# RWKV-6 attention and a channel MLP on one core: TensorE's order written out, the MLP in steps between the levels

## The chip, the core and the metric

The kernel runs on one core of one Trainium2 chip. The metric is the device time of one execution in microseconds. TensorE (PE, with its weight loads as PEld) multiplies and transposes, VectorE (DVE), ScalarE (ACT) and GpSimd (POOL) do the elementwise work, SyncE (SP) issues most DMAs. Each engine runs its own instructions strictly in the order in which they were laid down for it; engines wait for each other by semaphores.

## The reference, cut to what matters

```python
# r, k, v, w: (4, 8, 768, 48) float32; u: (8, 48); d_model 384, hidden 1536
for t in range(S):                                  # attention, per batch and head
    cur = einsum('bhd,bhe->bhde', u[None] * kt, vt)
    y[:, :, t] = einsum('bhd,bhde->bhe', rt, state + cur)
    state = wt[:, :, :, None] * state + einsum('bhd,bhe->bhde', kt, vt)
x = y.transpose(0, 2, 1, 3).reshape(B, S, H * D)    # 8 heads x 48 = 384
xn = (x - mean(x)) / sqrt(var(x) + 1e-06) * g_ln
out = x + maximum(xn @ w_ch1, 0.0) @ w_ch2
```

The weights `w_ch1` and `w_ch2` arrive as float64 and are converted on the chip.

## The kernel before, in words

A **round** is half a sequence of one batch (384 time steps, all 8 heads); there are 8 of them, numbered 0 to 7. A round has two **units** of 4 heads. Per unit `load` (L103) fetches w, k and r, `turned` (L226) transposes them on TensorE (`w_ps`, `k_ps`, `r_ps`) with ACT copying the results out (L236), `totals` (L238) multiplies the decays pairwise on POOL, and `own_term` (L254) makes the u-term on POOL and DVE.

`level` (L280) is run six times per round, for both units at once. Level `lev` multiplies with TensorE (`a_ps`, 48 products), then DVE scales `rT` and `kT` in place for the next level (L304, four multiplies) and copies the masked products into `A` (L317, two masked copies, not in the last level, where ACT copies at L315). So a level's products wait for DVE's multiplies of the level before. After the last level `ends` (L327, `kn_ps`) transposes k back, `states` (L337, `kv` on TensorE, then a chain of small DVE operations at L360) carries the state from chunk to chunk, and `outputs` (L374) forms `y`.

`mlp` (L415) is the second half for one round: normalisation on DVE (L425 to L431), three groups of transposes (`xT_ps`, L439), then 36 products `h_ps` (L448) and 36 products `o_ps` (L457). In the trace each of these 72 products is two rows. It is a generator: each `yield` ends a step. `weights` (L188) is a generator too: each of its 24 steps converts one piece of the weights (two ACT, three DVE operations at L208, L212, L216, one POOL add at L220); `convert(n)` runs n steps.

Order: the loop of L498 to L533 lays round `rnd`'s levels, and between them round `rnd-1`'s states, outputs and MLP and round `rnd+1`'s transposes. The written order is a priority only: a scheduler orders each engine's instructions by it and by when it takes their inputs to be ready. Buffers: `ps_t` (2) for transposes, `ps_a` (2) for `a_ps`, `kv` and `y`, `ps_m` (2) for `xT_ps`, `h_ps` and `o_ps`.

## Time and profile before

| | |
|---|---|
| median of 3 runs | 666.06 us (664.53 to 671.01) |
| profiled execution, device time | 667.42 us |
| its span, first to last instruction | 665.7 us |
| TensorE busy | 603.3 us, 91% of the span |
| DVE, ACT, POOL busy | 300.4 us (45%), 193.3 us (29%), 145.4 us (22%) |
| mean granted TensorE clock | 0.93 of 2.4 GHz |
| chain that ended last | PE 79%, DVE 11%, issue 3%, DMA 3% |

Busy shares are means over very different stretches. The table by stretches below shows for each how long each engine was busy and which clock TensorE was granted (1.00 is 2.4 GHz, 0.50 is 1.2 GHz). A row of the chain gives start, duration, engine, output, line and number of merged instructions.

### The profile page before, as it was taken

What the parts mean: (1) busy time and instruction counts of PE and PEld (TensorE: products, weight loads), DVE (VectorE), ACT (ScalarE), POOL (GpSimd) and SP (SyncE); (2) the same over time, 40 slices, a digit from 0 to 9 for tenths busy, and PEclk for the clock granted to TensorE, in tenths of its full rate; (3) what the DMA queues carried; (4) which work ended last, traced back from release to release, by engine and by line L of the source; (5) the groups of instructions that cost most, each with busy time, mean ns of one, the idle gap of its engine ahead of it and who ended that gap; (6) DMA issues with size and microseconds to landing.
All of it is one profiled execution on the core that took longest, in us unless ns stands there. A gap on an engine that the chain in (4) does not pass through costs nothing.

```text
span 665.7 us, 19173 instructions
## 1 busy us (share of the span) xinstructions
PE 603.3 (91%) x8456; PEld 408.2 (61%) x8456; DVE 300.4 (45%) x683; ACT 193.3 (29%) x412; POOL 145.4 (22%) x195
## 2 busy tenths in 40 slices
PE   1785477999999999999999999999899989997997
PEld 0674365666756676566766675666656666664554
DVE  1589897736721486016731565035801491133000
ACT  3545345431323122231333123231323102321210
POOL 5837664540133004030133004030003000000000
PEclk9995576999999996999899998999999978998999
DMA  9845655611520035000530044001200000000000
GB/s 153 173 118 151 142 148 129 154 26 36 115 39 1 26 77 99 1 13 16 107 68 1 26 92 85 1 13 40 44 1 13 14 16 0 1 26 13 1 12 24
DMA packets 123251, 36.83 MB, mean 55 GB/s; under 512 B 116896, under 2 KB 120096, under 8 KB 123168
## 3 DMA queue, kind: packets, MB, share of 16 engines
q1 hardware_dynamic: 118368, 34.73, 23.8%
q10 hardware_dynamic: 4800, 0.89, 1.1%
q8 instruction: 66, 1.08, 0.7%
q14 instruction: 17, 0.14, 0.1%
HBM read 30.87 MB, written 4.72 MB: 53 GB/s over the span
## 4 chain that ended last, share of the span: by engine, by line
PE 79%; DVE 11%; issue 3%; DMA 3%; ACT 2%; POOL 1%; SPq 1%; ACTq 0%; DVEq 0%; POOLq 0%
PE h_ps L448 29%; PE o_ps L457 28%; PE a_ps L294 9%; PE xT_ps L439 2%; PE kv L348 2%; DVE kT L304 2%; DVE rT L304 2%; PE w_ps L232 2%; DVE A L317 2%; PE kn_ps L334 2%; PE r_ps L232 1%; PE k_ps L232 1%; PE y L387 1%; DVE stats L426 1%; PE y L403 1%
## 5 line engine op out<-in xcount | busy, mean ns | idle before, releaser
L448 PE MATMUL h_ps<-xT,w_sb 128*128 128x384 f32 x576 | 196.1, 502 | 0.0
L457 PE MATMUL o_ps<-w_sb,h 128*128 128x384 f32 x576 | 195.0, 490 | 0.0
L448 PEld LDWEIGHTS h_ps<-xT,w_sb 128*128 128x128 f32 x576 | 112.6, 198 | 77.7 <-issue 7.1
L457 PEld LDWEIGHTS o_ps<-w_sb,h 128*128 128x128 f32 x576 | 106.6, 190 | 68.1
L294 PE MATMUL a_ps<-rT,kT 48*64 48x32 f32 x4608 | 101.5, 236 | 11.3 <-DVE kT L304 6.4
L294 PEld LDWEIGHTS a_ps<-rT,kT 48*64 48x64 f32 x4608 | 91.0, 153 | 32.7 <-issue 16.7
L304 DVE TENSOR_TENSOR rT<-rT,tot 128x384 f32<-128x384 f32 x80 | 49.8, 623 | 128.5 <-PE a_ps L294 128.0
L452 ACT ACTIVATE h<-h_ps 128x384 f32<-128x384 f32 x96 | 47.0, 489 | 133.7 <-PE h_ps L448 133.5
L464 DVE TENSOR_TENSOR o<-o_ps,x 128x384 f32<-128x384 f32 x24 | 13.4, 559 | 123.7 <-PE o_ps L457 123.7
L275 POOL TENSOR_TENSOR vo<-v,own 128x576 f32<-128x576 f32 x16 | 19.8, 1239 | 178.2 <-DMA v<-in_v_dram 165.4
L317 DVE COPY_PREDICATED A<-mask,a_ps 128x384 f32<-128x384 int8 x80 | 54.8, 749 | 0.0
L304 DVE TENSOR_TENSOR kT<-kT,tot 128x384 f32<-128x384 f32 x80 | 53.2, 666 | 0.0
L360 DVE SCALAR_TENSOR_TENSOR s<-s,decay,kv 128x48 f32<-128x48 f32 x160 | 29.4, 258 | 25.4 <-PE kv L348 25.4
L250 POOL TENSOR_TENSOR tot<-wT 128x384 f32<-128x384 f32 x16 | 14.8, 926 | 110.5 <-DVE kT L304 110.5
L220 POOL TENSOR_TENSOR w_sb<-we,wl 128x384 int32<-128x384 int32 x24 | 28.5, 1196 | 33.3 <-DVE we L216 24.7
L259 POOL TENSOR_TENSOR rk<-nat_k,nat_r 128x576 f32<-128x576 f32 x16 | 26.3, 1644 | 41.7 <-DMA nat_r<-in_r_dram 16.0
L369 ACT COPY sx<-s 64x288 f32<-64x288 f32 x32 | 13.8, 430 | 73.7 <-DVE s L360 73.4
L270 DVE TENSOR_REDUCE own<-rk 128x12 f32<-128x576 f32 x16 | 12.0, 749 | 46.2 <-POOL rk L264 46.2
L335 ACT COPY kn<-kn_ps 128x384 f32<-128x384 f32 x32 | 14.0, 481 | 52.3 <-PE kn_ps L334 38.9
L232 PE MATMUL k_ps<-ident,nat_k 128*128 128x128 f32 x96 | 18.7, 341 | 10.5 <-ACT wT L236 10.5
L439 PE MATMUL xT_ps<-ident,xn 128*128 128x128 f32 x72 | 18.7, 373 | 10.1 <-DVE xn L431 9.0
L403 PE MATMUL y<-sx,rx 48*64 48x48 f32 x384 | 24.5, 222 | 1.8 <-issue 1.8
(57 smaller groups left out, 599.4 us busy)
## 6 DMA issues: line engine op xcount, KB each, us to landing
raw<-in_moe_w_ch_dram SPq DMA_DIRECT2D x24, 384.0 KB, 3.6
v<-in_v_dram SPq DMA_DIRECT2D x64, 72.0 KB, 2.4
out_dram<-o SPq DMA_DIRECT2D x24, 192.0 KB, 1.9
nat_w<-in_w_dram SPq DMA_DIRECT2D x60, 72.0 KB, 2.9
nat_k<-in_k_dram SPq DMA_DIRECT2D x60, 72.0 KB, 3.1
nat_r<-in_r_dram SPq DMA_DIRECT2D x60, 72.0 KB, 2.6
vx<-in_v_dram SPq DMA_DIRECT2D x64, 36.0 KB, 2.3
nat_w<-in_w_dram ACTq DMA_DIRECT2D x4, 72.0 KB, 3.4
```

Source lines behind the costliest of these rows:

```text
L220: POOL.tensor_tensor(out=dst.bitcast(I32), in0=e, in1=low, op=ALU.add)
L232: PE.transpose(ps[:, ts(c, P)], nat[nm][q % 2][:, pr * TT + c].rearrange("p j d -> p (j d)"), ident,)
L259: POOL.tensor_tensor(out=rk, in0=nat["k"][q % 2][:, :, :, 0:D], in1=nat["r"][q % 2][:, :, :, 0:D], op=ALU.mult,)
L294: PE.matmul(ps[ds(C * (i ^ j), C), j, uu, c].rearrange("s (q n) -> s q n", n=n), K[rows, ts(m, C)], R[rows, m, :, 1, :], start=True, stop= ...
L304: DVE.tensor_tensor(out=X, in0=X, in1=T[:, :, 1 - i][:, :, None].broadcast_to(blocks), op=ALU.mult,)
L317: DVE.copy_predicated(out=out_j[:, :, 1, :], mask=masks[lev], data=ps_j)
L360: DVE.scalar_tensor_tensor(out=s[:, pr, m, :], in0=s[:, pr, m - 1, :] if m else before[:, pr, 2 * TT - 1, :], scalar=a["T"][NLEV][:, c : c ...
L403: PE.matmul(y[ds(C * i, C), j, k_], R, s, start=False, stop=True, skip_group_check=True,)
L439: PE.transpose(ps[:, ts(i, P)], xn[i].rearrange("p h d -> p (h d)")[:, ts(kc, P)], ident)
L448: PE.matmul(ps, w1_sb[:, kc, ts(f, P)], xT[:, kc, :], start=kc == 0, stop=kc == KC - 1)
L452: ACT.activation(out=hs[f], in_=ps, func=AF.Relu)
L457: PE.matmul(ps.rearrange("p h d -> p (h d)"), hs[f][:, ts(i, P)], w2_sb[:, f, :], start=f == 0, stop=f == FC - 1,)
```

## The change

- All TensorE instructions are kept in the written order (`keep_in_program_order`); the scheduler still places the other engines' instructions.
- Round 0 runs alone: levels, `ends`, `states`, `outputs`, normalisation and `xT` of its MLP are laid down before round 1's first level, with only round 1's transposes between them.
- The MLP's products are handed out by `fill` as 24 steps of three products. MLP 0 is spread over 11 levels (round 1's six and round 2's first five), every later MLP over six levels, and the transposes of the next round, of `kn` and of `xT` go one by one between these steps.
- `norm`, `turned_x` and `mlp` are separate; `xT_ps` uses `ps_t`; `ends` moves to the last level of its own round; the last level's ACT copies are collected in `late` and laid down by `finish`.
- The masks are kept once (32 columns) and broadcast when read; POOL makes them instead of ACT. The first loads go to SP and, for one of six, to ACT; the square root's table is loaded at the start. The converter's buffers come from the pool of `h`. Weights are converted three pieces per level from round 1.

```diff
+    def matmul(*args, **kw):
+        tc.keep_in_program_order(PE.matmul(*args, **kw))
+
+    def transpose(*args):
+        tc.keep_in_program_order(PE.transpose(*args))
...
-    load(0)
-    load(1, ACT)
+    load(0, (SP, SP, ACT))
+    load(1)
+    eps = const.tile([P, 1], F32, name="eps")
+    DVE.memset(eps, 1e-6)
+
+    ACT.activation(out=const.tile([P, 1], F32, name="root"), in_=eps, func=AF.Sqrt)
...
-        half = const.tile([P, U * NK, C // 2], I8, name=f"mask{lev}")
+        half = const.tile([P, C // 2], I8, name=f"mask{lev}")
...
-            ACT.copy(
-                out=half[rows],
-                in_=m[rows, None, ds(C // 2 * i, C // 2)].broadcast_to([C, U * NK, C // 2]),
-            )
...
+            POOL.tensor_copy(out=half[rows], in_=m[rows, ds(C // 2 * i, C // 2)])
...
-                    ACT.copy(out=out_j[rows, :, 1, :], in_=ps_j[rows])
+                    late.append((out_j[rows, :, 0, 1, :], ps_j[rows, :, 0]))
...
-                DVE.copy_predicated(out=out_j[:, :, 1, :], mask=masks[lev], data=ps_j)
+                mask = masks[lev][:, None].broadcast_to([P, U * NK, C // (2 * n), n])
+                DVE.copy_predicated(out=out_j[:, :, :, 1, :], mask=mask, data=ps_j)
...
-    MLP_STEPS = 2 + FC + TT * ((FC - 1) // 3 + 1)
+    MLP_STEPS = FC + TT * (FC // KC)
...
+    def fill(until, tasks):
+
+        n = int(until) - done
+        for i in range(max(n, len(tasks))):
+            if i < len(tasks):
+                tasks[i]()
+            for _ in range((i + 1) * n // max(n, len(tasks)) - i * n // max(n, len(tasks))):
+                mlp_step()
...
+    for part, nm in ((0, "w"), (1, "k"), (2, "r"), (3, None)):
+        (states if part < U else outputs)(now[part % U])
+        if nm:
+            for task in all_turned(new, nm):
+                task()
+    norm(0)
+    for task in all_x(0):
+        task()
...
+    FIRST = 2 * NLEV - 1
+    for rnd in range(1, NR + 1):
+        old, now, new = units_of(rnd - 1), units_of(rnd), units_of(rnd + 1)
         for lev in range(NLEV):
...
+            slot = (rnd - 1) * NLEV + lev + 1
+            until = MLP_STEPS * (
+                slot / FIRST if slot <= FIRST else 1 + (slot - FIRST) / NLEV
+            )
+            if rnd > 1 and lev < 2 * U:
+                (states if lev < U else outputs)(old[lev % U])
+                if lev == 2 * U - 1:
+                    norm(rnd - 1)
...
+            if lev == 4:
+                if rnd > 1:
+                    tasks = all_x(rnd - 1)
...
+            if lev == 5 and now:
+                tasks = [lambda: None] * 2 + all_ends(now)
+            fill(until, tasks)
+            if lev == 4 and rnd > 1:
+                mlps.append(mlp(rnd - 1))
```

**ACT at the start of the program, before** (`nat_` are the loaded operands, `mask_` the masks, `wT` the transposed decays of unit 0):

```order
L106 DMA nat_r_90<-in_r_dram 128x3x48 x4
L162 ACT_TABLE_LOAD
L162 COPY mask_148<-mask_0_144 64x384 x2
L162 COPY mask_155<-mask_1_151 64x384 x2
L162 COPY mask_162<-mask_2_158 64x384 x2
L162 COPY mask_169<-mask_3_165 64x384 x2
L162 COPY mask_176<-mask_4_172 64x384 x2
L236 COPY wT_183<-w_ps_0_184 128x384
L236 COPY wT_183<-w_ps_1_189 128x384
```

ACT at the start of the program, now:

```order
L112 DMA nat_r_89<-in_r_dram 128x3x48 x4
L135 ACT_TABLE_LOAD
L135 ACTIVATE root<-eps 128x1
L241 COPY wT_185<-w_ps_0_186 128x384
L241 COPY wT_185<-w_ps_1_191 128x384
```

Eight of ACT's twelve transfers have gone to SP, and ten mask copies stand no longer ahead of the first copy of a transposed operand.

**TensorE from MLP 0's last transpose on, before** (`a_ps_4` is level 4 of round 1):

```order
L439 MATMUL xT_ps_0_2_1350<-ident,xn_0_2_1324 128x128
L448 MATMUL h_ps_0_0_1377<-xT_0_1325,w_sb 128x384 x3
L448 MATMUL h_ps_0_1_1383<-xT_0_1325,w_sb 128x384 x3
L448 MATMUL h_ps_0_2_1474<-xT_0_1325,w_sb 128x384 x3
L448 MATMUL h_ps_0_3_1480<-xT_0_1325,w_sb 128x384 x3
L448 MATMUL h_ps_0_4_1528<-xT_0_1325,w_sb 128x384 x3
L448 MATMUL h_ps_0_5_1534<-xT_0_1325,w_sb 128x384 x3
L448 MATMUL h_ps_0_6_1540<-xT_0_1325,w_sb 128x384 x3
L294 MATMUL a_ps_4_1576<-rT_631,kT_534 64x32 x24
L294 MATMUL a_ps_4_1576<-rT_642,kT_545 64x32 x24
```

TensorE from MLP 0's last transpose on, now (`a_ps_0` is round 1's level 0, `w_ps` belongs to round 2):

```order
L59 MATMUL xT_ps_2_1071<-ident,xn_0_2_1045 128x128
L56 MATMUL a_ps_0_1116<-rT_972,kT_903 64x32 x24
L56 MATMUL a_ps_0_1116<-rT_983,kT_914 64x32 x24
L56 MATMUL h_ps_0_0_1195<-xT_1060,w_sb 128x384 x3
L56 MATMUL h_ps_0_1_1201<-xT_1060,w_sb 128x384 x3
L56 MATMUL a_ps_1_1237<-rT_972,kT_903 64x32 x24
L56 MATMUL a_ps_1_1237<-rT_983,kT_914 64x32 x24
L59 MATMUL w_ps_0_1293<-ident,nat_w_85 128x128 x3
L59 MATMUL w_ps_1_1298<-ident,nat_w_85 128x128 x3
L56 MATMUL h_ps_0_2_1303<-xT_1060,w_sb 128x384 x3
```

Before, four levels of round 1 had been laid down ahead of MLP 0 and its steps followed in one piece; now MLP 0's transposes stand ahead of all of round 1's levels, and two steps stand between two levels.

**TensorE in round 2 between levels 3 and 4, before**:

```order
L294 MATMUL a_ps_3_2316<-rT_1497,kT_1366 64x32 x24
L232 MATMUL r_ps_0_2390<-ident,nat_r_89 128x128 x3
L232 MATMUL r_ps_1_2395<-ident,nat_r_89 128x128 x3
L294 MATMUL a_ps_4_2443<-rT_1486,kT_1355 64x32 x4
L232 MATMUL r_ps_0_2401<-ident,nat_r_90 128x128 x3
L294 MATMUL a_ps_4_2443<-rT_1486,kT_1355 64x32
L232 MATMUL r_ps_1_2406<-ident,nat_r_90 128x128 x3
L294 MATMUL a_ps_4_2443<-rT_1486,kT_1355 64x32 x19
```

The same place now (`o_ps` are MLP 0's products):

```order
L56 MATMUL a_ps_3_2262<-rT_1557,kT_1428 64x32 x24
L59 MATMUL r_ps_0_2328<-ident,nat_r_89 128x128 x3
L59 MATMUL r_ps_1_2333<-ident,nat_r_89 128x128 x3
L56 MATMUL o_ps_0_1_2054<-w_sb,h_0_9_1675 128x384
L56 MATMUL o_ps_0_1_2054<-w_sb,h_0_10_1736 128x384
L56 MATMUL o_ps_0_1_2054<-w_sb,h_0_11_1753 128x384
L59 MATMUL r_ps_0_2345<-ident,nat_r_90 128x128 x3
L59 MATMUL r_ps_1_2350<-ident,nat_r_90 128x128 x3
L56 MATMUL o_ps_0_2_2355<-w_sb,h_0_0_1199 128x384
```

Before, only transposes stood between the two levels, since MLP 0's products had all been laid down by then; now two steps of MLP 0 stand there.

## Rows read from the trace of the kernel before

**Rows 1.** Page, part 1: busy us of TensorE, share, instructions.

```profile
PE 603.3 (91%) x8456; PEld 408.2 (61%) x8456; DVE 300.4 (45%) x683; ACT 193.3 (29%) x412; POOL 145.4 (22%) x195
```

**Rows 2.** Table by stretches: limits, length, busy us (instructions) by engine, clock, DMA.

```profile
core 0: us, PE busy (x) PEld busy (x) DVE busy (x) ACT busy (x) POOL busy (x), PEclk, DMA share, GB/s
0.00:29.00 29.00, 10.76 (x82) 7.77 (x83) 8.79 (x12) 13.47 (x27) 19.00 (x42) 1.00 1.07 175
29.00:109.00 80.00, 54.86 (x1281) 46.07 (x1282) 72.03 (x144) 36.38 (x79) 45.24 (x44) 0.68 0.54 134
109.00:184.00 75.00, 73.86 (x1162) 49.43 (x1162) 45.94 (x101) 25.61 (x56) 23.42 (x27) 0.98 0.41 89
184.00:258.00 74.00, 72.97 (x1046) 49.29 (x1044) 31.02 (x77) 19.95 (x44) 13.14 (x19) 0.94 0.22 45
...
551.00:614.00 63.00, 58.09 (x552) 36.58 (x551) 14.46 (x46) 15.06 (x32) 0.00 (x0) 0.96 0.03 11
```

**Rows 3.** Chain that ended last, one round and the end: start, us, what.

```profile
183.66 23.41 PE h_ps L448 x72
207.07 1.53 PE a_ps L294 x96
...
231.89 0.84 PE kv L348 x48
...
234.12 1.49 PE o_ps L457 x4
237.16 2.78 PE o_ps L457 x8
239.94 0.66 PE w_ps L232 x6
...
551.35 21.94 PE h_ps L448 x66
...
614.04 24.95 PE h_ps L448 x72
639.00 23.23 PE o_ps L457 x72
```

**Rows 4.** Table by stretches, at one end of a round (columns as above).

```profile
249.00:262.00 13.00, 13.00 (x131) 9.04 (x127) 9.47 (x18) 3.84 (x8) 4.15 (x3) 0.50 0.65 123
```

**Rows 5.** Timeline at the start (start, us, queue); last row: page 6, us to landing.

```profile
10.32 1.28 ACT L162 ACT_TABLE_LOAD   x1 [10.32 <-DMA nat_r<-in_r_dram]
11.62 3.11 ACT L162 COPY mask<-mask 64x384 int8<-64x384 int8 x6
...
17.01 0.86 ACT L236 COPY wT<-w_ps 128x384 f32<-128x384 f32 x2
...
19.60 1.97 SPq L106 DMA_DIRECT2D nat_k<-in_k_dram  x4
...
nat_r<-in_r_dram SPq DMA_DIRECT2D x60, 72.0 KB, 2.6
```

**Rows 6.** Groups by line, DVE: count, busy us, mean ns, idle before.

```profile
L317 DVE COPY_PREDICATED A<-mask,a_ps 128x384 f32<-128x384 int8 x80 | 54.8, 749 | 0.0
L304 DVE TENSOR_TENSOR kT<-kT,tot 128x384 f32<-128x384 f32 x80 | 53.2, 666 | 0.0
L212 DVE TENSOR_SCALAR we<-we 128x384 int32<-128x384 int32 x24 | 14.1, 592 | 0.2
```

**Rows 7.** Timeline, DVE's first levels and POOL beside them.

```profile
29.03 0.87 DVE L304 TENSOR_TENSOR rT<-rT,wT 128x384 f32<-128x384 f32 x1 [1.18 <-PE a_ps L294]
...
32.62 1.77 DVE L304 TENSOR_TENSOR kT<-kT,wT 128x384 f32<-128x384 f32 x1
...
36.96 0.55 DVE L304 TENSOR_TENSOR kT<-kT,tot 128x384 f32<-128x384 f32 x1
...
32.54 1.43 POOL L259 TENSOR_TENSOR rk<-nat_k,nat_r 128x576 f32<-128x576 f32 x1 [0.48 <-DMA nat_r<-in_r_dram]
```

**Rows 8.** Waits of TensorE: for whom, us in total, times, longest.

```profile
PE xT_ps L439 <- DVE xn L431: 9.0, 5, 4.7
```

More of the change, by code (lines that the diff above doesn't have):

```diff
@@ L224, with turned @@
     st, carry = {}, {}
[L226 removed]
+    def turned(q, nm, pr):
         a = st.setdefault(q, {})
[L228 to L236 removed]
+        if pr == 0:
+            a[nm] = (p2 if nm == "w" else p4).tile([P, W], F32, tag=nm, name=f"{nm}T{q}")
+        ps = ps_t.tile([P, RN], F32, tag="t", name=f"{nm}_ps{q}_{pr}")
+        for c in range(TT):
+            transpose(
+                ps[:, ts(c, P)],
+                nat[nm][q % 2][:, pr * TT + c].rearrange("p j d -> p (j d)"), ident,
+            )
+        ACT.copy(out=a[nm][:, ts(pr, RN)], in_=ps)
     def totals(q):
@@ L478, in convert, with mlp_step @@
             next(ws, None)
-    for q in range(U):
+    mlps, done = [], 0
+    def mlp_step():
+        nonlocal done
+        while mlps:
+            if next(mlps[0], mlps) is not mlps:
+                done += 1
+                return True
+            mlps.pop(0)
+        return False
+    def fill(until, tasks):
[5 more added lines that the diff above has]
+                mlp_step()
@@ L481, with all_turned, all_ends, all_x @@
+    def all_turned(qs, nm):
+        return [lambda q=q, pr=pr: turned(q, nm, pr) for q in qs for pr in range(NP)]
+    def all_ends(qs):
+        return [lambda q=q, pr=pr: ends(q, pr) for q in qs for pr in range(NP)]
+    def all_x(rnd):
+        return [lambda kc=kc: turned_x(rnd, kc) for kc in range(KC)]
+    def units_of(rnd):
+        return [U * rnd + g for g in range(U)] if rnd < NR else []
+    now, new = units_of(0), units_of(1)
+    for q in now:
         for nm in "wkr":
-            turned(q, nm)
+            for task in all_turned([q], nm):
+                task()
@@ L483 @@
         totals(q)
-    for q in range(U):
+    for q in now:
         own_term(q)
-    mlps, owed = [], 0.0
-    def mlp_steps(n):
-        nonlocal owed
-        owed = owed + n if mlps else 0.0
-        while mlps and owed >= 1.0:
-            if next(mlps[0], mlps) is mlps:
-                mlps.pop(0)
-            else:
-                owed -= 1.0
-    RATE = 1.05 * MLP_STEPS / NLEV
-    for rnd in range(NR + 1):
-        now, old, new = (
-            [U * i + g for g in range(U)] if 0 <= i < NR else [] for i in (rnd, rnd - 1, rnd + 1)
-        )
-        for lev in range(NLEV):
-            if old and lev == 0:
-                for q in old:
-                    ends(q)
-            if old and lev in (0, 1):
-                states(old[lev])
+    for lev in range(NLEV):
+        level(now, lev)
+        if lev == 0:
+            for q in now:
+                load_vx(q)
+        if lev == 1:
+            for q in new:
+                load(q)
+        convert(2)
@@ L517 @@
                     load(q)
-            if lev in (1, 2, 3):
-                for q in new:
-                    turned(q, "wkr"[lev - 1])
+            tasks = []
+            if new and lev in (1, 2, 3):
+                tasks = all_turned(new, "wkr"[lev - 1])
             if lev == 3:
```

128 lines of the change are left out of this document (65 added, 63 removed).

## The prediction

> **What bounds the kernel now.** I read the page's busy line first: TensorE is busy 91% of the span [rows 1]. That is a mean, so the table by stretches comes next, and there three regimes are to be seen [rows 2]. Up to 29 us almost nothing but loading happens, with the DMA engines full. From 29 to 109 us DVE is the bound, 72.0 of 80 us, while TensorE has 54.9, mostly at 1.2 GHz (clock 0.68): the only TensorE work at hand is that of the levels, whose products each wait for DVE. From 109 us on, when MLP 0's products are there, TensorE is busy nearly throughout. The chain then shows what one round is made of [rows 3]: from 183.66, where MLP 1's products begin, to 239.94 it is dense; behind that the MLP has run out, and the rest of the round is levels and transposes that wait for DVE, with pauses, and in the round shown with the clock at 0.50 for 13 us although TensorE counts as fully busy [rows 4]. At the round's end TensorE waits for the normalisation, 9.0 us over five places [rows 8].
>
> From 183.66 to MLP 6's start at 551.35 there are five rounds, 73.5 us each; MLP 6's round has 62.7, and MLP 7 48.2 up to the last product at 662.2 [rows 3]. Behind that are 3.5 us to the end of the span at 665.7, and 1.7 us lie between the span and the device time of 667.4. The profiled execution is 1.4 us above the median of 666.06.
>
> **The start.** ACT copies the first transposed operand at 17.01: until 10.32 it stood behind its own loads, then came the table and ten mask copies [rows 5]. DVE's first level began at 29.03 [rows 7]. Now ACT issues 4 transfers and copies at once. Unit 1's r, the last operand that level 0 needs, is the twentieth transfer on SP; four took 1.97 us there [rows 5], so issuing ends at some 11 us, landing 2.6 later [rows 5] at 13.5, and two transposes, a copy and half a level put DVE's first multiply at about **17 us** (estimate): 12 earlier.
>
> The Trainium skill, page "Trainium Kernel Development and Optimization", Key Constraints, says that transfers from all queues share the same 16 DMA engines and that more issuing engines save only issue time. By it the move of transfers from ACT to SP brings no datum earlier; the trace agrees as far as it goes, with a DMA share of 1.07 from both queues in the first stretch [rows 2].
>
> Up to MLP 0's products DVE has the work of the stretch from 29 to 109 without two parts: four of round 1's levels, which now stand behind MLP 0's transposes, and four of 16 conversions (12 are laid down ahead now). A level has four multiplies of 0.67 and two masked copies of 0.75 [rows 6], 4.1 us; a conversion has three operations of about 0.59, 1.77 us. So 72.0 - 16.4 - 7.1 = 48.5 us of DVE remain; at the same nine tenths busy that is 54, and I add 6 for the chain `kn`, `kv`, `y`, normalisation, `xT`, which has no level beside it any more. MLP 0 starts at 17 + 54 + 6 = **77 us** instead of 109 (bounds 70 and 84).
>
> **Eleven levels beside MLP 0.** Now two or three of MLP 0's 24 steps stand between two levels. A step is three products, 6 rows; 72 rows take 23.41 us [rows 3], so 1.95. TensorE's part of one of the first five levels is 1.53 + 3.9 + 1.3 for transposes (six take 0.66, 239.94 in rows 3) and some joints, 7.1 us. DVE's is 4.1 + three conversions, 5.3, together 9.4 in four of the five: there DVE stays the bound, and the early start is partly waited away. 8 + 4 x 9.4 = 45.6. With these pauses the clock is open; the nearest rows are 0.68 [rows 2] and 0.50 [rows 4]. Never low costs nothing; always low makes a level 14 us of TensorE, 19 more in four. I take 6. The sixth level has three steps and `kn`, 9 us. The next five hold 11 steps (21.5), levels 7.6, `kv` 1.7, two `y` at 1.55 (the gap before 237.16 in rows 3) plus joints 3.5, transposes 5.2: 39.5, and 3 where the normalisation joins the level on DVE. So the point that stood at 183.66, MLP 0 done and level 4 of round 2 too, comes at 77 + 51.6 + 9 + 42.5 = **180 us** (160 to 204). The start gains 3 us only: MLP 0 no longer runs in one dense piece.
>
> DVE's own operations are the softest number. One multiply took 1.77 us while POOL's 1.43 ran beside it, another 0.55 [rows 7]. Without such meetings DVE's part falls below TensorE's and the point comes near 160. The Trainium skill, page "SBUF — State Buffer", Who interferes with whom, says that DVE and GpSimd share a port pair as an exclusive lock, so that the later one waits for the whole of the other's instruction. The trace agrees in that one meeting (0.55 + 1.2 against 1.77). If each of the 12 POOL adds of the conversions beside these levels held DVE up by that 1.2, the sum would be some 14 us longer.
>
> **The rounds behind it.** One round at full clock without pauses is 56.3 (183.66 to 239.94) plus what is left: three levels 4.6, transposes 4.0, a `y` 1.75, `xT` 1.0: 67.6. So 4 x 67.6, one round without new transposes at 63.6, MLP 6's round with 56 and MLP 7 with 46.6 are 436.6, against 478.6 now: 42 us lie in these ends of rounds. The order now puts four steps, 7.8 us, between any two levels, and the next MLP begins at level 5 where the last one ends at level 4; so the wait for DVE (4.1 us per level, 31.0 per round of 74 [rows 2]) has cover, and without cover it would be back. I give back 6 for some ten more joints per round (about 0.12 each, from 1.49 for four `o_ps` rows against 0.32 each) and 9 for the level with the normalisation, and for ACT's copies at the sixth, 1.5 per round. Gain **27 us**: 451.6 remain.
>
> Costed at nothing: the broadcast mask (same element count; if its reading doubled the copy, 1.5 us in each of 10 DVE-bound levels, 15 us, otherwise covered); ten small copies on POOL, about 0.52 each by ACT's 3.11 for six [rows 5], ahead of work that starts at 7 us; `kn` at two buffers; out transfers, which wait behind loads on SP but have two buffers. The square root's table, 1.28 us at 10.32 [rows 5], is loaded ahead of the work.
>
> **Sum.** 180 + 451.6 + 3.5 = 635 us of span, 637 with the 1.7 outside it.
>
> **Rivals.**
> - *DVE does not bind in the first levels.* For it speaks 0.55 us per multiply alone [rows 7]; against it the mean of 0.67 over all rounds [rows 6]. The point comes at 160: 617 us.
> - *The strict order brings the wait back.* A TensorE instruction that waits now holds up everything behind it, MLP steps too; before, the scheduler had placed the products behind the levels. The place is the level with the normalisation: DVE has a `y` addition, the normalisation and four multiplies there, about 8 us (estimate, operations of 0.5 to 0.8), against 10.6 on TensorE (1.53 + 7.8 + 1.3). Meetings with POOL, or ACT's copies at the sixth level, could turn that into 3.5 to 4 us of pause per round, 22 in all: 659 us, hardly a change.
> - *The clock falls in every round* (the other side). At 249 us it was at 0.50 with TensorE fully busy on transposes and levels [rows 4]; these now stand in among the steps. For 13 us per round at half clock 6.5 us are lost, 39 in six rounds: 676 us, slower. It decides from 6 us per round on. Against it: the dense part of rows 3 has levels, `kv` and `y` between pieces of 1.5 to 9 us of MLP and ran at the price of full clock.
>
> **How the numbers follow.** A change under 1% can't be told from none here, so the limits are 659.4 and 672.7. Forecast 0.64, DVE not binding 0.17, wait brought back 0.12, clock in every round 0.07. Nearly all of the first, all of the second and a third of the third are faster: 0.81; the rest of the third and some of the first within 1%: 0.12; slower 0.07. The range goes from 614 (first rival, less 3) to 664 (start at its upper bound, 24 more, or the strict order's 659 with some of it); the clock's case is left out.
>
> **What would show it.** In the profile after: DVE's first level near 17 us; MLP 0's first product near 77 and MLP 1's near 180; DVE busy nine tenths up to 130; in the later rounds TensorE busy over 97% with clock near 1.00 and rounds of about 70 us instead of 73.5; the wait of `xT_ps` for DVE nearly gone. Wrong would be: a new wait of `a_ps` or `kn_ps` of more than 2 us per round; a clock under 0.9 in rounds 3 to 7; or a start of MLP 1 beyond 200, which would mean that the spread of MLP 0 costs more than the earlier start gives.

## The result, and the profile after

The changed kernel takes 629.41 us (median of 4 runs, 629.00 to 630.72), against 665.82 us for the kernel before, run beside it (664.53 to 671.01): a ratio of 0.945, with a 95% interval of 0.940 to 0.950. Medians, here and below, are of all runs of a kernel; ratios leave out the runs of a slower state, more than 1.5% above the kernel's fastest, which the kernel before and e4 show. The forecast was 637 us, between 614 and 664. The profiled execution of after has a span of 628.1 us.

Engines' busy time (page, part 1), to be laid beside [rows 1]:

```profile
PE 573.4 (91%) x8456; PEld 387.2 (62%) x8456; DVE 303.2 (48%) x683; ACT 185.2 (29%) x402; POOL 152.4 (24%) x205
```

TensorE's share is the same 91%, which shows how little that number says. Its 8456 products and transposes are the same, and their busy time fell from 603.3 to 573.4 us; idle time fell only from 62.4 to 54.7. Most of the gain is TensorE being quicker at the same work.

Stretches of after, cut at the marks that the forecast used (first product of MLP 0, of MLP 1, then round by round; columns as in [rows 2]):

```profile
0.00:17.00 17.00, 9.70 (x132) 6.83 (x132) 2.73 (x3) 7.03 (x14) 12.61 (x45) 1.00 0.79 141
17.00:85.00 68.00, 37.71 (x901) 32.28 (x901) 55.36 (x116) 26.28 (x56) 42.73 (x43) 0.59 0.66 152
85.00:182.00 97.00, 88.75 (x1598) 61.26 (x1595) 69.77 (x141) 35.89 (x80) 44.83 (x38) 0.92 0.47 104
182.00:254.00 72.00, 69.53 (x1051) 46.55 (x1052) 34.90 (x83) 20.55 (x45) 13.28 (x18) 0.98 0.23 49
254.00:321.00 67.00, 67.00 (x1066) 45.41 (x1065) 33.30 (x75) 20.03 (x45) 13.41 (x18) 1.00 0.25 50
321.00:389.00 68.00, 67.11 (x1050) 45.35 (x1048) 33.69 (x79) 19.74 (x45) 13.16 (x18) 1.00 0.24 49
524.00:578.00 54.00, 54.00 (x453) 33.42 (x452) 11.41 (x40) 14.50 (x32) 0.00 (x0) 1.00 0.03 10
```

From MLP 1 on TensorE hardly rests and holds 2.4 GHz. Ahead of MLP 0 the picture is the old one: DVE busy 55.4 of 68 us, TensorE mostly at 1.2 GHz.

Chain that ended last, marks of after (start, us, what), beside [rows 3]:

```profile
85.39 6.61 PE h_ps L56 x12
...
181.91 2.15 PE h_ps L56 x6
184.61 1.94 PE h_ps L56 x6
...
253.64 2.13 PE h_ps L56 x6
...
578.18 23.22 PE h_ps L56 x72
601.40 23.23 PE o_ps L56 x72
```

MLP 0 begins at 85.4 (before some 109), MLP 1 at 181.9 (183.7), and the last product ends at 624.6 (662.2). So only 2 us are won up to MLP 1, and 36 behind it: 442.7 us remain from there instead of 478.5.

The same two stretches, before (184 to 662) and after (182 to 625):

```profile
184.00:662.00 478.00, 463.63 (x5934) 304.92 (x5932) 173.12 (x427) 117.88 (x253) 57.75 (x84) 0.96 0.14 30
```

```profile
182.00:625.00 443.00, 437.25 (x5838) 286.81 (x5838) 175.08 (x425) 115.97 (x252) 52.25 (x80) 0.99 0.14 31
```

The idle part went from 14.4 to 5.8 us, the busy part from 463.6 to 437.3, with 1.6% fewer records in the second (one level of round 2, some 1.5 us, stands ahead of MLP 1's start now). Part of the difference is the clock, 0.96 against 0.99. An estimate: if a mean of 0.96 stands for 8% of the time at half clock and 0.99 for 2%, that is up to 19 and 4 us lost, so up to 15 of the 26. The rest shows in a round of before that had full clock throughout, from MLP 3's start to MLP 4's. TensorE is busy for 69.7 us there; the same round of after, 321 to 389 above, has as many records and needs 67.1:

```profile
335.00:406.00 71.00, 69.72 (x1050) 47.01 (x1049) 31.64 (x79) 20.29 (x44) 13.15 (x18) 1.00 0.26 52
```

What TensorE does there in before, at the end of the MLP (timeline, PE; two transposed operands and levels 2 and 3 in turns):

```profile
396.57 0.39 PE L294 MATMUL a_ps<-rT,kT 48*64 48x32 f32 x10 [0.20 <-DVE A L317]
396.89 0.87 PE L232 MATMUL k_ps<-ident,nat_k 128*128 128x128 f32 x6
397.69 1.48 PE L294 MATMUL a_ps<-rT,kT 48*64 48x32 f32 x86
399.10 0.87 PE L232 MATMUL r_ps<-ident,nat_r 128*128 128x128 f32 x6
400.52 0.32 PE L294 MATMUL a_ps<-rT,kT 48*64 48x32 f32 x8 [0.54 <-DVE kT L304]
400.77 0.55 PE L232 MATMUL r_ps<-ident,nat_r 128*128 128x128 f32 x3
401.24 0.30 PE L294 MATMUL a_ps<-rT,kT 48*64 48x32 f32 x2
```

Levels are broken up between transposes: 8 rows of `a_ps` take 0.32 us there, while an unbroken level of 96 takes 1.39 to 1.6, so 8 would be 0.13. The end of one row overlaps the next, so starts are the better measure: 0.25 us from the start of the 8 rows to that of the transposes, and 0.47 for the three transposes, which take 0.33 between steps of the MLP (step 5 further down). The break costs some 0.26 us. In the trace behind MLP 1's start `a_ps` stands in 63 pieces for 31 levels before, and now in one piece per level but for a few rows beside `y`; at 0.2 to 0.26 us for each of 32 breaks that is 6 to 8 us (estimate). With the clock's 15 and the level's 1.5 that makes most of the 26. The groups of TensorE's rows from MLP 1's start to the last product point the same way, though they hold the clock's part too; before, then after (columns as in [rows 6]):

```profile
L294 PE MATMUL a_ps<-rT,kT 48*64 48x32 f32 x2976 | 61.1, 227 | 5.0 <-DVE A L317 3.0 <-DVE mv L427 0.9 <-DVE kT L304 0.5
L439 PE MATMUL xT_ps<-ident,xn 128*128 128x128 f32 x55 | 14.6, 374 | 6.1 <-DVE xn L431 5.5 <-ACT xT L442 0.2
```

```profile
L56 PE MATMUL a_ps<-rT,kT 48*64 48x32 f32 x2888 | 50.0, 219 | 4.4 <-issue 4.4
L59 PE MATMUL xT_ps<-ident,xn 128*128 128x128 f32 x54 | 9.1, 278 | 0.0
```

### The profile page after: what moved, and what is told of

It is laid out like the page before. It is cut to its first block, busy times and chain, and to the rows that moved or that the text cites. A ratio compares the mean times of both kernels' runs of the same rounds, so it can differ in the third digit from the quotient of the medians.

```text
span 628.1 us, 19238 instructions
## 1 busy us (share of the span) xinstructions
PE 573.4 (91%) x8456; PEld 387.2 (62%) x8456; DVE 303.2 (48%) x683; ACT 185.2 (29%) x402; POOL 152.4 (24%) x205
## 4 chain that ended last, share of the span: by engine, by line
PE 82%; DVE 8%; issue 3%; DMA 2%; POOL 2%; SPq 2%; ACT 1%; POOLq 0%; DVEq 0%; ACTq 0%
PE h_ps L56 30%; PE o_ps L56 29%; PE a_ps L56 10%; PE y L56 4%; PE kv L56 2%; PE r_ps L59 2%; PE kn_ps L59 2%; SPq L112 2%; DVE we L221 1%; PE w_ps L59 1%; PE xT_ps L59 1%; DMA nat_r<-in_r_dram 1%; DVE kT L309 1%; PE k_ps L59 1%; DVE rT L309 1%
## 5 line engine op out<-in xcount | busy, mean ns | idle before, releaser
L56 PE MATMUL h_ps<-xT,w_sb 128*128 128x384 f32 x576 | 202.1, 499 | 2.2 <-ACT h L475 2.2
L56 PE MATMUL o_ps<-w_sb,h 128*128 128x384 f32 x576 | 201.2, 495 | 0.0
L56 PEld LDWEIGHTS o_ps<-w_sb,h 128*128 128x128 f32 x576 | 106.4, 194 | 61.3 <-issue 3.0
L56 PE MATMUL a_ps<-rT,kT 48*64 48x32 f32 x4608 | 86.8, 229 | 25.8 <-DVE kT L309 20.2
L56 PEld LDWEIGHTS a_ps<-rT,kT 48*64 48x64 f32 x4608 | 81.2, 146 | 37.4 <-issue 19.7
L309 DVE TENSOR_TENSOR kT<-kT,tot 128x384 f32<-128x384 f32 x80 | 60.2, 752 | 0.0
L421 DVE TENSOR_TENSOR x<-y,vo 128x576 f32<-128x576 f32 x16 | 12.1, 757 | 61.6 <-PE y L56 61.6
L460 ACT ACTIVATE xT<-xT_ps,g_sb 128x384 f32<-128x384 f32 x24 | 13.9, 580 | 58.5 <-PE xT_ps L59 58.5
L241 ACT COPY rT<-r_ps 128x384 f32<-128x384 f32 x32 | 14.6, 477 | 50.7 <-PE r_ps L59 50.7
L241 ACT COPY kT<-k_ps 128x384 f32<-128x384 f32 x32 | 14.8, 478 | 43.9 <-PE k_ps L59 43.8
L56 PEld LDWEIGHTS y<-v,A 64*64 64x64 f32 x384 | 21.8, 138 | 8.1 <-issue 7.1
```

Of the source, the lines that this page charges most:

```text
L56: tc.keep_in_program_order(PE.matmul(*args, **kw))
L241: ACT.copy(out=a[nm][:, ts(pr, RN)], in_=ps)
L309: DVE.tensor_tensor(out=X, in0=X, in1=T[:, :, 1 - i][:, :, None].broadcast_to(blocks), op=ALU.mult,)
L460: ACT.activation(out=xTs[rnd][:, kc, :], in_=ps, func=AF.Copy, scale=g_sb[:, kc : kc + 1])
```

## The experiments

"First level" is DVE's first multiply, "rest" the time from MLP 1's first product to the end of the last product, all from one profile each; times are medians. Kernels whose code ahead of MLP 0 is the same as after's begin it at 85.4, 88.6 and 88.8, and e2, whose code is that of after up to MLP 1, begins MLP 1 at 185.1 instead of 181.9: a mark is good to about 3 us. Each ratio is to the kernel before as run beside that kernel. There were three such groups after the first comparison, each on a chip of its own: e1 to e4; e5, e9, e11, e12; e6, e7, e20, e22. After itself was run in none of them, and the kernel before has medians of 664.57 to 667.11 in them. So a difference of 3 or 4 us between kernels of different groups, or to after, is not shown by the medians alone.

| kernel | time, us | ratio to before (95%) | first level | MLP 0 | MLP 1 | rest |
|---|---|---|---|---|---|---|
| before | 665.82 | 1 | 29.0 | 108.7 | 183.7 | 478.5 |
| after | 629.41 | 0.945 (0.940 to 0.950) | 24.1 | 85.4 | 181.9 | 442.7 |
| e1_free_order | 630.57 | 0.956 (0.950 to 0.961) | 18.1 | 87.1 | 183.1 | 439.9 |
| e2_one_piece | 711.47 | 1.078 (1.071 to 1.084) | 24.0 | 88.8 | 185.1 | 521.3 |
| e11_mlp0_behind | 641.00 | 0.968 (0.962 to 0.974) | 24.1 | 126.0 | 197.0 | 441.7 |
| e6_mlp0_dense | 640.54 | 0.964 (0.959 to 0.969) | 24.1 | 93.7 | 195.8 | 440.5 |
| e3_old_start | 634.23 | 0.962 (0.957 to 0.967) | 31.0 | 96.4 | 191.1 | 438.7 |
| e4_new_start_alone | 664.16 | 0.997 (0.991 to 1.003) | 18.1 | 108.5 | 186.8 | 479.9 |
| e5_own_later | 621.84 | 0.940 (0.935 to 0.944) | 15.6 | 83.1 | 177.3 | 439.8 |
| e22_own_pinned | 625.21 | 0.940 (0.935 to 0.946) | 24.1 | 84.2 | 179.5 | 439.5 |
| e7_conversion_cut | 627.93 | 0.944 (0.939 to 0.949) | 24.1 | 88.6 | 183.0 | 440.9 |
| e9_convert_later | 630.48 | 0.953 (0.948 to 0.958) | 24.1 | 82.4 | 185.2 | 439.1 |
| e12_both | 630.21 | 0.952 (0.948 to 0.958) | 15.6 | 80.2 | 184.4 | 439.0 |
| e20_raw_ahead | 631.88 | 0.950 (0.943 to 0.956) | 15.6 | 86.2 | 192.7 | 439.0 |

The kernel before scatters more than after (657 to 685 us in the later comparisons), which widens the intervals. The profiles of e11 (643.89 us) and e20 (637.19) are of the slowest of their runs, that of e4 (671.94) is of one near its slowest.

### Are the steps between the levels what counts, or the pins?

**e2_one_piece:** MLP 1 to 7 in one piece each; everything else, pins too, as in after.

```diff
-                slot / FIRST if slot <= FIRST else 1 + (slot - FIRST) / NLEV
+                slot / FIRST if slot <= FIRST else 1 + -(-(slot - FIRST) // NLEV)
```

> MLP 1 to MLP 7 are handed out in one piece of 24 steps at the slot where the next one of the six begins, instead of four steps per level; MLP 0 as it was. Theory (an uncovered level waits for DVE): five of six gaps between levels have no TensorE work but transposes, DVE's 4.1 us per level show as waits of a_ps, less the 0.7 to 1.3 us of transposes: some 12 us per round over six rounds with levels beside them, 680 to 705 us. Rival (what counts is that TensorE's order is pinned and the next MLP begins at level 5; the waits would be short because DVE works ahead of TensorE): under 645 us.

Measured 711.47 us, 82 more than after and more than the kernel before. MLP 1 begins at 185.1, and the rest is 79 us longer. The stretch from MLP 1's start to the last product, and one end of a round:

```profile
185.10:706.40 521.30, 481.24 (x5844) 323.35 (x5838) 171.43 (x425) 116.93 (x252) 51.25 (x80) 0.90 0.12 26
```

```profile
235.00:265.00 30.00, 23.39 (x874) 20.50 (x866) 25.32 (x71) 9.02 (x20) 2.67 (x2) 0.89 0.41 80
```

The theory is right against the rival, but its sum is not: it had some 12 us of waits in each of six rounds and nothing for slower products. In the 30 us without steps DVE is busy for 25.3 and TensorE for 23.4. Over the whole rest TensorE is idle for 40 us instead of 5.8 and busy for 44 us longer, at a clock of 0.90. Of the waits of `a_ps`, 13.0 us are put down to DVE's chain of states `s`, 3.7 to its multiplies and 1.6 to its masked copies: it is DVE's whole work between two levels that shows, and not the multiplies alone. So an uncovered level is paid for twice, about half in waits and half in slower products; and the pinned order without the steps is worse than what the free scheduler made of the kernel before.

**e1_free_order:** the pins taken away, the order still written as in after.

```diff
-        tc.keep_in_program_order(PE.matmul(*args, **kw))
+        PE.matmul(*args, **kw)
...
-        tc.keep_in_program_order(PE.transpose(*args))
+        PE.transpose(*args)
```

> Only the pins are taken away: TensorE's instructions are written in the same order, but the scheduler may move them again. Theory (the gain of the later rounds comes from steps of the MLP standing between the levels; the pin only keeps what is written): the scheduler moves some transposes and levels forward, most steps stay between the levels: 625 to 645 us. Rival (the pin carries the gain, since a free scheduler gathers the MLP's products into one dense piece again, as in the kernel before): rounds go back towards 73 us, 650 to 665 us, with a_ps waiting for DVE again by 4 us at several levels of each round.

Measured 630.57 us (628.19 to 631.97): by the medians no difference that these runs can tell from after's 629.00 to 630.72. The ratios, 0.956 and 0.945, would allow the pins some 7 us (estimate), their intervals just touch. The theory is right, the rival out: the rest is 439.9 us, no longer than after's. The scheduler leaves the steps where they are written; the clearest move is at the start, where it takes most of two levels of round 1 ahead of MLP 0's transposes. The pin is not where the gain comes from.

One thing stays open. The kernel before was not in one piece: its steps stood between levels until they ran out. How much of the 36 us is the even spread, and how much the rest of TensorE's new order (transposes one by one between steps, `ends` in its own round, `xT_ps` in other buffers), was not run apart.

### What the first MLP's place is worth

**e11_mlp0_behind:** round 0's states, outputs and normalisation between round 1's levels, MLP 0 over six levels, as in later rounds.

```diff
-    for part, nm in ((0, "w"), (1, "k"), (2, "r"), (3, None)):
-        (states if part < U else outputs)(now[part % U])
...
-    mlps.append(mlp(0))
...
-                slot / FIRST if slot <= FIRST else 1 + (slot - FIRST) / NLEV
+                max(0, slot - NLEV + 1) / NLEV
...
-            if rnd > 1 and lev < 2 * U:
+            if lev < 2 * U:
```

> Changed kernel without the first MLP's chain ahead of round 1's levels: round 0's states, outputs, normalisation and transposes stand between round 1's first five levels as in later rounds, and MLP 0 is handed out over six levels instead of eleven. Theory (round 1's first five levels then have no steps beside them and are bound by DVE at about 9 us each, while the chain of states is covered): MLP 0's first product at 112 to 122 us, MLP 1's 6 to 12 us later than 181.9, time 635 to 642 us. Rival (the place of that chain is worth nothing, TensorE's total work up to MLP 1 decides): 627 to 632 us. Rival (the uncovered levels cost as much as in the kernel before, and MLP 1 begins near 195 or later): 643 us or more.

Measured 641.00 us, 11.6 more than after, as the theory had it. The marks are later than it said: MLP 0 at 126.0, and MLP 1 15 us later, where the second rival saw it (195 or later), though that rival's time of 643 us or more was not reached. Ahead of MLP 0 DVE is now the bound for a long stretch:

```profile
17.00:126.00 109.00, 60.62 (x1421) 51.05 (x1421) 95.86 (x183) 42.58 (x92) 60.71 (x59) 0.57 0.64 152
```

So the early chain of round 0, together with the eleven levels over which it lets MLP 0 be spread, is worth about a third of the gain, although MLP 1's start hardly moved against the kernel before.

**e6_mlp0_dense:** MLP 0 over round 1's six levels instead of eleven, and what that needs from the converter.

```diff
-                slot / FIRST if slot <= FIRST else 1 + (slot - FIRST) / NLEV
+                min(1, slot / NLEV) if slot <= FIRST else 1 + (slot - FIRST) / NLEV
...
-            convert(3)
+            convert(4)
...
-            e = ph.tile([P, WC], I32, tag="h", name=f"we{i}")
-            low = ph.tile([P, WC], I32, tag="h", name=f"wl{i}")
+            e = p2.tile([P, WC], I32, tag="we", name=f"we{i}")
+            low = p2.tile([P, WC], I32, tag="wl", name=f"wl{i}")
```

> Changed kernel with MLP 0 handed out over the six levels of round 1 (four steps each) instead of over eleven; round 2's first five levels then have no steps beside them, as the forecast's first MLP in one dense piece had none behind it. Four pieces of weights per level in round 1, the converter's buffers its own. Theory (the eleven levels are better covered by a spread MLP 0; five uncovered ones cost some 2 to 4 us each, less what DVE's work in round 1 costs now): MLP 1's first product 5 to 15 us later than 181.8, 634 to 645 us. Rival (work done earlier is not lost; TensorE's total up to MLP 1 decides): 627 to 631 us.

Measured 640.54 us, inside the theory's range. But of the 14 us by which MLP 1 is late, 8 lie ahead of MLP 0 (the converter has two buffers of its own instead of a share of thirteen; on the same code marks differ by 3 us). From MLP 0 to MLP 1 it is 102.1 us instead of 96.5, but that these 6 us are the price of the dense MLP 0 is not shown: e9 below keeps the spread, has the same two buffers (and conversions laid down later) and takes 102.8. What the trace shows is the levels of round 2 without steps, with 6.3 of 50 us idle and a clock of 0.80; the last 52 us of after ahead of MLP 1 are in the second line:

```profile
146.00:196.00 50.00, 43.70 (x1053) 34.34 (x1052) 32.33 (x77) 14.95 (x33) 9.66 (x16) 0.80 0.30 61
130.00:182.00 52.00, 49.27 (x1002) 35.05 (x1001) 34.14 (x73) 14.48 (x33) 16.38 (x20) 0.95 0.31 62
```

### What the start is worth, and what holds DVE's first level

**e3_old_start:** the first loads, the table and the masks as in the kernel before.

```diff
-    load(0, (SP, SP, ACT))
-    load(1)
+    load(0)
+    load(1, (ACT, ACT, ACT))
...
-    ACT.activation(out=const.tile([P, 1], F32, name="root"), in_=eps, func=AF.Sqrt)
...
-            POOL.tensor_copy(out=half[rows], in_=m[rows, ds(C // 2 * i, C // 2)])
+            ACT.copy(
+                out=half[rows],
+                in_=m[rows, None, ds(C // 2 * i, C // 2)].broadcast_to([C, U * NK, C // 2]),
+            )
```

> The changed kernel with the start of the kernel before: unit 1 loaded by ACT, the root's table not ahead of the work, full masks copied by ACT. Theory (the first level of DVE moves by the amount that ACT's first copy moves, some 5 to 10 us, and most of it is waited away in round 1 and MLP 0): 632 to 638 us, DVE's first level near 29 us, MLP 1's first product 3 to 8 us later than 181.9. Rival (the start reaches the end in full): 638 to 642 us. Rival (the start is worth nothing, DVE's order holds the first level back anyway): within 1 us of 629.4.

Measured 634.23 us (633.36 to 636.80), 4.8 more than after: the first theory. The first level comes 7 us later, MLP 1 9 us later (the theory had 3 to 8), and 4 of these are back by the end, since this profile's rest is that much shorter than after's.

**e4_new_start_alone:** the other side, the kernel before with only this start.

```diff
-    load(0)
-    load(1, ACT)
+    load(0, (SP, SP, ACT))
+    load(1)
...
+    ACT.activation(out=const.tile([P, 1], F32, name="root"), in_=eps, func=AF.Sqrt)
...
-                DVE.copy_predicated(out=out_j[:, :, 1, :], mask=masks[lev], data=ps_j)
+                mask = masks[lev][:, None].broadcast_to([P, U * NK, C // (2 * n), n])
+                DVE.copy_predicated(out=out_j[:, :, :, 1, :], mask=mask, data=ps_j)
```

> The kernel before with the new start alone (loads by SP, table at the start, masks once by POOL and broadcast when read). Theory (the start alone gains little, since MLP 0 then begins earlier but the rounds behind it keep their ends without cover): the first level some 5 us earlier and 3 to 6 us off the time, 660 to 663 us. Rival (the start is the gain, the order of TensorE is not): 640 us or less. Rival (a masked copy with a broadcast mask costs more where DVE binds): 666 us or more, with masked copies above 0.80 us.

Measured 664.16 us, a ratio of 0.997 (0.991 to 1.003). A gain of 3 to 6 us lies within that interval, none does too; 640 is out. The start is not the gain. In its one profile DVE's first level comes at 18.1, 11 us earlier than before, and yet MLP 0 at 108.5 (108.7 before): as far as that profile tells, the early start was waited away. The masked copies take 746 ns on average, against 749 before, so the second rival is out too.

**e5_own_later:** in after DVE's first level is not at 17 us, although its operands were there. Timeline of after, DVE, then POOL, then TensorE:

```profile
17.49 0.75 DVE L275 TENSOR_REDUCE own<-rk 128x12 f32<-128x576 f32 x1 [13.32 <-POOL rk L269]
23.48 0.75 DVE L275 TENSOR_REDUCE own<-rk 128x12 f32<-128x576 f32 x1 [5.23 <-POOL rk L269]
24.14 0.55 DVE L309 TENSOR_TENSOR rT<-rT,wT 128x384 f32<-128x384 f32 x1
```

```profile
16.06 1.40 POOL L269 TENSOR_TENSOR rk<-rk,u_bc 128x576 f32<-128x576 f32 x1 [1.88 <-DMA u_bc<-in_u_dram]
18.32 1.40 POOL L264 TENSOR_TENSOR rk<-nat_k,nat_r 128x576 f32<-128x576 f32 x1 [0.87 <-DVE own L275]
```

```profile
14.52 1.60 PE L56 MATMUL a_ps<-rT,kT 48*64 48x32 f32 x96
25.25 1.51 PE L56 MATMUL a_ps<-rT,kT 48*64 48x32 f32 x48 [9.13 <-DVE kT L309]
```

Level 0's products are done at 16.1. But the two reductions of the own term stand ahead of the level in DVE's order, and the second waits for POOL, which waits for the first (one buffer `rk`). The edit lays round 0's own term down behind level 1 and keeps the reductions at their written place:

```diff
-        DVE.tensor_reduce(
+        tc.keep_in_program_order(DVE.tensor_reduce(
...
-    for q in now:
-        own_term(q)
     for lev in range(NLEV):
         level(now, lev)
+        if lev == 1:
+            for q in now:
+                own_term(q)
```

> Changed kernel; round 0's own term is laid down behind level 1 and its two reductions keep their written place on DVE, so that they no longer stand ahead of DVE's first level waiting for POOL. Theory (operands were ready; the reductions alone hold the first level from 16 to 24 us, and DVE binds until MLP 0 begins, so most of it reaches the end, less what round 1 waits away): DVE's first level at 16 to 18 us, MLP 0's first product 5 to 8 us earlier than 85.4, time 621 to 626 us. Rival (the later part of the start is bound elsewhere, by raw weights, v or POOL, so that the gain is waited away before MLP 0): 627 to 630 us. Rival (the reductions' wait only moves to another place of DVE's order): 629 us or more.

Measured 621.84 us (620.29 to 624.04): the theory's time, 7.6 under after and the lowest median of the study. By the ratios, 0.940 against 0.945, it is some 3.5 us (estimate), with intervals that overlap. The first level comes at 15.59:

```profile
15.59 0.56 DVE L309 TENSOR_TENSOR rT<-rT,wT 128x384 f32<-128x384 f32 x1 [11.42 <-PE a_ps L56]
16.06 1.75 DVE L309 TENSOR_TENSOR kT<-kT,wT 128x384 f32<-128x384 f32 x1
```

But the way was another one. MLP 0 begins at 83.1, only 2 us earlier, which is within what marks scatter, so of 8.5 us more than 6 are waited away ahead of it, as the first rival said. e1 has the same: first level at 18.1, MLP 0 at 87.1. From first level to MLP 0 DVE has as much work in e5 as in after (55.0 and 54.2 us), but takes 67.5 us for it instead of 61.3, and among its waits are 6.4 us for the converter's operations on ACT:

```profile
15.60:83.10 67.50, 38.33 (x944) 32.69 (x937) 55.01 (x112) 25.77 (x56) 35.40 (x40) 0.56 0.67 156
```

**e22_own_pinned:** the same pin with nothing moved.

```diff
-        DVE.tensor_reduce(
+        tc.keep_in_program_order(DVE.tensor_reduce(
```

> Changed kernel with only the own term's reductions kept at their written place on DVE, in all rounds, and none of them moved: the other half of the faster version, in which round 0's own term is also laid down later. Theory (the later first level is what costs; it stays near 24 us here): 626 to 630 us, the gain of 7.5 us being mostly that of the move. Rival (the gain lies in the later places, where the scheduler had put reductions ahead of round 0's chain of states and of levels, waiting for POOL): 620 to 625 us with DVE's first level still near 24 us.

Measured 625.21 us (621.31 to 627.32), with the first level still at 24.1: at the border of both ranges, so the medians don't decide. The ratio is that of e5, 0.940, so that the earlier first level is worth anything on top of the pin is not shown; by the medians, from two different groups, it would be 3 us. That the pin alone gains something is likely (4 us by the median, 3 by the ratio), but not where. By the profiles the last product ends at 619.0, against 624.6 in after and 617.1 in e5; the rest of 439.5 is that of e5, but also that of e1, e3 and e7 (438.7 to 440.9), which have no such pin. At the end of round 0's levels a reduction waits 3.1 us ahead of the chain of states in after; in e22 it no longer stands there, but DVE waits 4.4 us for TensorE's `kv` instead, and MLP 0 begins at 84.2.

### Does DVE bind beside MLP 0?

**e7_conversion_cut:** two of three DVE operations left out of the last 12 conversions.

```diff
-            DVE.tensor_scalar(
+            if i < len(parts) // 2:
+                DVE.tensor_scalar(
```

> The last 12 of 24 weight conversions, those beside round 1's levels, leave out two of three DVE operations, so this part of the weights' conversion is not done; 12 x 2 operations of about 0.59 us, 14 us of DVE, fall away there. Forecast's theory (in round 1's levels DVE is the bound at 9.4 us against 7.1 on TensorE): four levels become some 2.3 us shorter each, MLP 1's first product near 173 instead of 181.8, time 619 to 622 us. Rival (with steps of the MLP beside them these levels wait for DVE hardly at all, as 3.6 us of waits of a_ps between 80 and 185 us suggest): at most 4 us, 625 to 629 us.

Measured 627.93 us (624.95 to 629.07), 1.5 under after: the rival. From MLP 0 to MLP 1 it is 94.4 us instead of 96.5, with DVE busy for 63.9 us instead of 69.8. So the edit took 5.8 us of DVE's time away and not 14: the 24 operations are gone, but others became longer (the conversion's last one, L221 in after, takes 859 ns on average instead of 548). It is a weaker test than it was meant to be:

```profile
88.50:183.00 94.50, 85.04 (x1589) 58.57 (x1582) 63.94 (x117) 35.73 (x80) 37.66 (x37) 0.96 0.47 102
```

**e9_convert_later** takes work out of the stretch ahead of MLP 0 and puts it here; **e12_both** does so on top of e5.

```diff
-        convert(2)
+        convert(1)
...
-            e = ph.tile([P, WC], I32, tag="h", name=f"we{i}")
-            low = ph.tile([P, WC], I32, tag="h", name=f"wl{i}")
+            e = p2.tile([P, WC], I32, tag="we", name=f"we{i}")
+            low = p2.tile([P, WC], I32, tag="wl", name=f"wl{i}")
```

> Changed kernel with one instead of two weight pieces converted per level of round 0 (6 instead of 12 ahead of MLP 0, the other six in two more levels behind its start; the converter's buffers are its own again, two each). Theory (DVE binds from 17 us to MLP 0, six conversions are 10.6 us of its work): MLP 0 begins 6 to 10 us earlier; its first levels carry three conversions in six levels instead of four and give part of it back: 621 to 627 us. Rival (DVE binds in round 1 as well, at 9.4 us per level, so that work moved there comes back in full): 628 to 632 us. Rival (conversions come too late for MLP 0's second half, or two buffers are too few): 633 us or more.

> The last two edits together. Theory (both take DVE time out of the stretch ahead of MLP 0): gains add up to about 10 us, 615 to 622 us. Rival (the same stretch can only be shortened once, down to what transposes, v and the chain of states need): no better than the better one of the two, within 2 us.

Measured 630.48 and 630.21 us. In e9 that is the first rival's range. e12 is 8.4 us above e5, which neither its theory nor its rival (within 2 us of the better one) allowed for. MLP 0 begins 3 us earlier in each than without the edit, and MLP 1 3 to 7 us later. Waits of TensorE in e12 between 80 and 150 us (for whom, us, times, longest):

```profile
PE kn_ps L59 <- DVE kT L309: 4.6, 1, 4.6
PE a_ps L56 <- DVE s L374: 2.6, 1, 2.6
PE k_ps L59 <- ACT kT L241: 2.5, 1, 2.5
PE r_ps L59 <- ACT rT L241: 1.8, 1, 1.8
PE w_ps L59 <- ACT wT L241: 1.6, 1, 1.6
```

More conversions beside the levels do cost, as e9's first rival said, but in part as waits for ACT's copies, which stand behind the converter's operations in ACT's order. The work came back in full and more. Whether the two buffers or the later conversions do it is left open, since the edits weren't run apart; ahead of the late copies in e12 the converter waits on ACT once for POOL to give a buffer back (3.4 us) and twice for raw weights (1.8 and 1.2 us). What can be said is that DVE's work beside MLP 0 has little room upwards, and that taking some away (e7) gives next to nothing.

**e20_raw_ahead:** e5 with round 1's loads two levels later, so that raw weights pass them on SP.

```diff
-        if lev == 1:
+        if lev == 3:
             for q in new:
                 load(q)
```

> The faster version (own term pinned, round 0's laid down later) with round 1's loads of w, k and r laid down two levels later, so that transfers of raw weights stand ahead of or between them on SP. Theory (the converter starves, since ACT waits 13.3 us once for raw weights that stand on SP behind loads waiting for a free buffer; DVE idles 3 us behind it twice): 616 to 620 us. Rival (DVE's other work and the chain of states set the pace, the converter has time): 621 to 623 us. Rival (round 1's transposes become late): 624 us or more.

Measured 631.88 us, 10 more than e5: the third rival's time. Its reason is not shown. MLP 0 begins 3 us later than in e5, with one wait of 2.7 us for a transposed operand of round 1, and 12 us more come between MLP 0 and MLP 1 (192.7), where TensorE is busy for 93.0 of 106.5 us at a clock of 0.88, against 84.6 of 94.2 at 0.97 in e5.

## Why the prediction came out as it did, step by step

The total was 8 us too high. The mechanism it named for the gain, the MLP's steps as cover for levels and transposes behind MLP 1's start, is what e2 shows, and e1 that the pins are not needed for it. Its terms erred in both directions.

1. **"DVE's first multiply at about 17 us."** 24.1. Loads, copies and products came as worked out (the last operand landed at 13.9, against 13.4 in the kernel before, copies of transposed operands run from 5.4 on, level 0's products are done at 16.1), but the step followed the operands alone and not DVE's order, in which reductions waiting for POOL stood ahead. e5 moves them and has 15.6.
2. **"MLP 0 starts at 77"**, bounds 70 and 84. 85.4, past the bound. From the first level it is 61.2 us, against 54 + 6 = 60 in the sum, DVE nine tenths busy as assumed, so that the whole error seems to be that of step 1. But e5 and e1 show that the sum would have failed with an early first level too: there 67.5 and 69 us follow, not 60. The step that failed is that an earlier first level moves MLP 0 by as much. With this start and order MLP 0 begins at 83 to 89 us whether the first level comes at 15.6 (e5, e20), 18.1 (e1) or 24.1 (after and the kernels with its start); what holds it is open.
3. **Eleven levels: 51.6 + 9 + 42.5 = 103 us.** 96.5. The mis-sized term is "8 + 4 x 9.4" for levels bound by DVE; the 6 for the clock was near (a mean of 0.92 over 97 us loses at most 7.8). TensorE waits only 3.6 us for DVE's multiplies there, and e7 shows that 24 operations fewer change next to nothing. DVE is busy for 69.8 of 97 us, and for 35.6 of the 45 up to 130, where the forecast saw nine tenths. That is so although its `kT` multiplies, meeting POOL, take 867 ns there on average, 18 of them, and not the 0.67 us of the sum. Here the first rival, "DVE does not bind", was right in its mechanism, and its price of 20 us was too high: TensorE's own work is 88.8 us of the stretch.
4. **MLP 1's first product at 180.** 181.9, since errors 2 and 3 nearly cancel (8.4 late, 6.5 early): that is luck. "The start gains 3 us only" holds (1.8), but the reason given, MLP 0 no longer in a dense piece, is not borne out: e6, with MLP 0 in six levels instead of eleven, takes no less time from MLP 0 to MLP 1, but 5.6 us more (with two buffers for the converter). A spread MLP 0 delays its own end, not TensorE's work.
5. **451.6 us remain.** 442.7. The 9 for stalls are mis-sized: TensorE waits 0.9 us for ACT at `kn` and 4.4 for nothing that the profile shows, in all six rounds (1.0 and 4.8 in e1, so this is not the pins' doing). "6 for some ten more joints" was a cost that doesn't exist. Three transposes between two steps cost what three transposes cost:

```profile
255.94 2.10 PE L56 MATMUL h_ps<-xT,w_sb 128*128 128x384 f32 x6
257.87 0.82 PE L59 MATMUL kn_ps<-ident,kT 128*128 128x128 f32 x6
258.53 2.10 PE L56 MATMUL h_ps<-xT,w_sb 128*128 128x384 f32 x6
260.47 0.49 PE L59 MATMUL kn_ps<-ident,kT 128*128 128x128 f32 x3
260.79 2.10 PE L56 MATMUL h_ps<-xT,w_sb 128*128 128x384 f32 x6
```

   A step starts 2.59 or 2.26 us after the one before it, with six or three transposes between: 1.94 + 0.66 or 0.33, as in [rows 3]. The joints that cost were in the kernel before, inside its broken levels. That reading, 6 to 8 us, rests on prices and counts and has no experiment of its own.
6. **Costed at nothing.** The broadcast mask is right: a masked copy took 749 ns on average before [rows 6] and takes 751 now. The ten small copies on POOL and the table at 2.97 us delay nothing that is late.
7. **The wait of `xT_ps`** for the normalisation, 9.0 us in [rows 8], is 5.7, all of it ahead of MLP 0; behind MLP 1's start there is none, as forecast.

The rivals: the strict order brings no wait back, since there is no wait for DVE behind 182 us. The clock's case is out for after (0.98 to 1.00 in every round), but e2 shows that it is real: the same pinned order without the steps runs the rest at 0.90. What decides is whether steps stand between the levels.

DVE and POOL meet, as the forecast's softest number feared. POOL in e5, beside the two rows of DVE above, and DVE's groups in after (columns as in [rows 6]):

```profile
15.99 1.41 POOL L269 TENSOR_TENSOR rk<-rk,u_bc 128x576 f32<-128x576 f32 x1 [2.00 <-DMA u_bc<-in_u_dram]
```

```profile
L309 DVE TENSOR_TENSOR kT<-kT,tot 128x384 f32<-128x384 f32 x80 | 60.2, 752 | 0.0
L323 DVE COPY_PREDICATED A<-mask,a_ps 128x384 f32<-128x384 int8 x80 | 54.6, 751 | 0.0
```

The multiply that begins at 16.06 takes 1.75 us and ends 0.41 behind POOL's operation; the one ahead of it took 0.56. Over the whole kernel the `kT` multiplies have a mean of 752 ns, against 666 before [rows 6]. The Trainium skill, page "SBUF — State Buffer", Who interferes with whom, says that a DVE instruction with two SBUF inputs contends with a GpSimd instruction that reads SBUF, and that issue order decides who is blocked. The traces agree in that meeting. From MLP 0's start on it costs little, as far as e7 shows that DVE doesn't bind there.

## What to carry to other kernels

Where two kinds of work alternate on an engine, one dense and one that waits for a second engine at each step, hand the dense one out in pieces between the waits: written in one piece it cost 82 us here, with the same instructions and the same pins. Look at such a change as a sum over TensorE's busy time as well as its waits: three quarters of the gain behind MLP 1 were products that ran faster, with idle time a quarter. And before costing "when the operands are there", read what stands ahead in the other engine's own order; a small reduction that waits for a third engine held DVE's first level for 8 us. Then read what comes next as well: of these 8 us, when they were won, hardly 2 reached MLP 0.

## What the runs showed of the hardware that was not expected

- A gap is paid for twice on TensorE. In the end of a round of e2 the granted clock falls to 0.89, with 6.6 of 30 us idle; over the whole rest 34 us more of waiting go with 44 us more of busy time for the same products.
- Changing between products of the MLP and transposes costs no measurable time (0.33 us for three transposes, from start to start), but a level's small products broken up between transposes do cost: in the case shown 8 rows and the three transposes behind them take 0.25 and 0.47 us from start to start, where 0.13 and 0.33 would be their share.
- A masked copy reads a mask that is broadcast over 12 blocks at the same price as a full one: 751 against 749 ns.
